# The first half of wq loaded by two DMAs, 16 partitions and then 112

## The chip, the cores and the metric

The kernel runs on one core of a Trainium2 chip. The metric is the device time of one execution in microseconds.

## The reference

One decoding step for 4 sequences: attention over a cache, and a small MLP mixer, both on the layer-normed input, summed. All data are float32.

```python
B, Sq, D = 4, 1, 512;  H, Sk, Dh = 32, 4096, 128;  F = 1792
xn = layernorm(x)
# A: attention with cached keys and values, each (4, 32, 4096, 128)
q = (xn @ wq).reshape(B, Sq, H, Dh).transpose(0, 2, 1, 3)     # wq (512, 4096)
scores = einsum("bhqd,bhkd->bhqk", q, k_cache) * Dh ** -0.5
o = einsum("bhqk,bhkd->bhqd", softmax(scores), v_cache)
A = o.transpose(0, 2, 1, 3).reshape(B, Sq, H * Dh) @ wo       # wo (4096, 512)
# B: with one token a sequence every spatial shift leaves zeros, so x1 = xn
Bm = xn + gelu(layernorm(xn) @ w3) @ w4                       # w3 (512, 1792), w4 (1792, 512)
out = x + A + Bm
```

## The kernel before

The two caches are 268 MB each and are read once. The kernel walks through them in 32 groups of 4 heads; a group's K is a tile of 128 partitions by 64 KB, and so is its V. Three buffers of that size (`slots`: S0, S1, S2) hold everything large. K of even groups goes to S1, of odd groups to S0, and V always to S2 (the last V to S1).

All large loads are issued by SP, in one order written out by hand, and so go through one DMA queue. First come the two halves of wq (line 132), 128 partitions by 32 KB each, into S2, each with a semaphore of its own (`s_wq[0]`, `s_wq[1]`); then the two halves of K(0) (line 127); then SP waits for `d_Q`, the signal that the query is ready, since K(1) goes to S0, where the work on the query lies. Then follow K(1) (L123), V(0) (L140), and V and K in turn, each as soon as its buffer is free: V(g) after `v_free`, which PE gives when it is done with the V before, and K(g+2) after `k_free`, which DVE gives when it is done with K(g). At the end come w3, w4 and wo, the last in six pieces (L152). The input x (4 rows of 2 KB, needed at four places) comes through ACT's queue (L226).

The query is made in the first 35 us. DVE norms x (L290 to L308), transposes it (L310), and PE multiplies it with wq. PE goes through wq in four chunks c, and waits for `s_wq[0]` ahead of chunk 0 and for `s_wq[1]` ahead of chunk 2. ACT scales the product (L232), DVE transposes it and copies it to `Q` (L318, L319), which sets `d_Q`.

In each group, DVE multiplies K with the query in two halves (L332, L334) and sums over the head dimension (L337), then takes the maximum (L339 to L342). ACT makes the exponentials (L242), and PE contracts them with V (`contract`) and sums the four quarters (`outputs`). After the last group, PE multiplies the result with wo as its pieces arrive, and DVE copies the sum out (L387).

The layout of a wq half is this: partition p holds rows 4p to 4p+3 of wq, and a half is two of these rows, 32 KB that lie together both in HBM and in the buffer.

Of the kernel before, what the change touches and what calls it, by code (L numbers as in the profile page):

```python
# [13 lines left out]
P = 128  # L14
# [6 lines left out]
def decode_block(ctx: ExitStack, tc: tile.TileContext, x, k, v, wq, wo, w3, w4, out):  # L21
# [4 lines left out]
    NC = D // P  # L26
# [39 lines left out]
    def sem(name):  # L66
        return tc.alloc_semaphore(name)

    def take(e, s, n=1):
        e.wait_ge(s, n).then_inc(s, -n)  # L70
# [4 lines left out]
    s_wq = [sem(f"swq{n}") for n in range(2)]  # L75
# [16 lines left out]
    def group(flat, g):  # L92
        n = HG * S * DH
        return flat[g * n:(g + 1) * n].rearrange("(p r) -> p r", p=P)
# [8 lines left out]
    wq_sb = S2[:, :].rearrange("p (c n) -> p c n", c=NC)  # L103
# [11 lines left out]
    def mm(e, o, l, r, start, stop):  # L115
        return e.matmul(o, l, r, start=start, stop=stop)  # L116

    with tc.tile_critical(no_gpsimd_drain=True), nc.Block(no_gpsimd_drain=True) as block:

        @block.sync  # L120
        def _(e):
            def load_k(g):
                e.dma_start(KS[g % 2][:, :], group(kf, g)).then_inc(s_k[g % 2], 16)  # L123

            def load_k_half(g, n, s):
                r = slice(n * ROW // 2, (n + 1) * ROW // 2)
                e.dma_start(KS[g % 2][:, r], group(kf, g)[:, r]).then_inc(s, 16)

            wq_r = wq.rearrange("(p c) n -> p c n", p=P)
            for n in range(2):  # L130
                c = slice(n * NC // 2, (n + 1) * NC // 2)
                e.dma_start(wq_sb[:, c, :], wq_r[:, c, :]).then_inc(s_wq[n], 16)
            load_k_half(0, 0, s_k[0])
            load_k_half(0, 1, s_kh)
            e.wait_ge(d_Q, 1)
            load_k(1)
            for g in range(NG - 1):
                if g > 0:
                    take(e, v_free)
                e.dma_start(S2[:, :], group(vf, g)).then_inc(s_v, 16)  # L140
                if g + 2 < NG:
                    take(e, k_free[g % 2])
                    load_k(g + 2)
            take(e, k_free[0])
            e.dma_start(S1[:, :], group(vf, NG - 1)).then_inc(s_vl, 16)
            take(e, v_free)
            e.dma_start(w3_sb, w3.rearrange("(p c) f -> p c f", p=P)).then_inc(s_w3, 16)
            e.dma_start(w4_sb, w4.rearrange("(p m) n -> p m n", p=P)).then_inc(s_w4, 16)
            take(e, k_free[1])
            wo_r = wo.rearrange("(p c) n -> p c n", p=P)  # L150
            for n, (c0, c1) in enumerate(PIECES):
                e.dma_start(wo_sb[:, c0:c1, :], wo_r[:, c0:c1, :]).then_inc(s_wo[n], 16)  # L152
# [12 lines left out]
        @block.tensor  # L165
        def _(e):
            e.wait_ge(d_xT, 1)
            for c in range(NC):
                if c % (NC // 2) == 0:
                    e.wait_ge(s_wq[c // (NC // 2)], 16)  # L170
                w = wq_sb[:, c, :].rearrange("p (n j h d) -> p n h j d", n=2, j=JB // 2, h=HG)
                for n in range(2):
                    for h in range(HG):
                        i = mm(e, (pa, pb)[n][32 * h:32 * h + 32, :], xnT[:, c, :], w[:, n, h], c == 0, c == NC - 1)
                    if c == NC - 1:
                        i.then_inc(p_q, 1)

            def contract(V):
                for g in range(G4):
                    t = g % 4  # L180
                    i = mm(e, pv[32 * t:32 * t + 32, :], pw[:, g, :], V[:, 4 * g:4 * g + 4, :], g < 4, g >= G4 - 4)
                return i

            def outputs(done):
                i = mm(e, oz[:, HG:2 * HG], ones[:, :], rs[:, :], True, True)
                if done is not None:
                    i.then_inc(done, 1)
                take(e, a_os)
                for m in range(4):
                    i = mm(e, oz[:, 0:HG], os[:, m, :], sel[:, HG * m:HG * m + HG], m == 0, m == 3)  # L190
                i.then_inc(p_oz, 1)

            def spread(b):
                take(e, d_lt)
                mm(e, pa[:, 32 * b:32 * b + 32], lt[:, :, :], sel[:, :], True, True).then_inc(p_x, 1)

            with nc.Fori(0, NG - 1, 1, engines=[ET.PE]):
                take(e, s_v, 16)
                take(e, a_w)
                contract(V3).then_inc(p_pv, 1)  # L200
                outputs(v_free)
            for b in range(B - 1):
                spread(b)
            take(e, a_w)
            e.wait_ge(s_vl, 16)
            contract(VL).then_inc(p_pv, 1)
            e.wait_ge(s_w3, 16)
            for c in range(NC):
                for t in range(4):
                    i = mm(e, pb[32 * t:32 * t + 32, :FT], x1T[:, c, :], w3_sb[:, c, t * FT:(t + 1) * FT],  # L210
                           c == 0, c == NC - 1)
            i.then_inc(p_up, 1)
            outputs(None)
            spread(B - 1)
            mm(e, total[:, 0:P], ident[:, :], base[:, :], True, False)
            e.wait_ge(s_w4, 16)
            e.wait_ge(d_g, 1)
            for m in range(NF):
                t = m % 4
                mm(e, y[32 * t:32 * t + 32, :], gT[:, 32 * m:32 * m + 32], w4_sb[:, m, :], m < 4, False)  # L220
# [145 lines left out]
    with tc.tile_critical(no_gpsimd_drain=True):  # L366
        e = nc.tensor
# [53 lines left out]
```

## Time and profile before

| | |
|---|---|
| time, median of 3 runs | 1305.53 us (1305.29 to 1305.79) |
| the profiled execution | 1305.59 us |
| its span | 1303.7 us |
| DVE busy | 1168.0 us, 90% |
| PE busy | 363.5 us, 28% |
| ACT busy | 98.6 us, 8% |
| SP's DMA queue | 561.00 MB, 99.5% of 16 engines' span |
| mean DMA rate | 430 GB/s |

The span is the time between the first and the last recorded instruction; the execution's time also has what lies around it. A busy time counts an engine's own instructions, not its waits. The share of the DMA queue is the time that its packets took, over the span of 16 DMA engines. "Landing" is the time from the issue of a transfer to the arrival of its last part, so it includes the time that the transfer stood in the queue behind others.

### The profile page before, as it was taken

How to read it: one execution, taken by the hardware profiler on the slowest of the kernel's cores; microseconds unless marked ns; L12 is line 12 of the kernel's file. 1: busy time of each engine (PE TensorE's matmuls, PEld its weight loads, DVE VectorE, ACT ScalarE, POOL GpSimd, SP SyncE). 2: the span in 40 equal slices, each digit the busy share in tenths (PEclk: the TensorE clock that was granted, in tenths of full speed). 3: DMA queues.
4: the chain of work that ended last, by engine and by line, in shares of the span. 5: the costliest groups of instructions: out<-in, count | busy, mean ns of one | idle time of the engine just before them, and what ended most of it. 6: DMA issues, size and time to landing. Idle time of an engine off the chain costs nothing. (4 is left out here: it accounts for less than half of the span.)

```text
span 1303.7 us, 7006 instructions
## 1 busy us (share of the span) xinstructions
PE 363.5 (28%) x2622; PEld 130.8 (10%) x2622; DVE 1168.0 (90%) x340; ACT 98.6 (8%) x334; POOL 2.1 (0%) x9
## 2 busy tenths in 40 slices
PE   3032123333113333213333212333311333321246
PEld 0010001111001111001111000111100111100112
DVE  3999999999999999999999999999999999999971
ACT  0000000000000000000000000000000000000010
POOL 0000000000000000000000000000000000000000
PEclk9565566666566666556666556666556666655669
DMA  9999999999999999999999999999999999999998
GB/s 403 435 445 424 444 422 442 426 440 426 436 432 432 436 430 438 424 444 422 446 422 446 423 440 426 438 430 438 428 438 430 430 438 428 440 424 444 422 431 342
DMA packets 10870, 561.11 MB, mean 430 GB/s; under 512 B 1232, under 2 KB 1248, under 8 KB 1520
## 3 DMA queue, kind: packets, MB, share of 16 engines
q1 hardware_dynamic: 10816, 561.00, 99.5%
q8 instruction: 3, 0.05, 0.0%
q10 hardware_dynamic: 48, 0.04, 0.0%
q14 instruction: 3, 0.02, 0.0%
HBM read 561.02 MB, written 0.01 MB: 430 GB/s over the span
## 5 line engine op out<-in xcount | busy, mean ns | idle before, releaser
L337 DVE TENSOR_REDUCE sc<-slot 128x128 f32<-128x16384 f32 x32 | 551.0, 17220 | 8.2 <-DVEq L70 8.2
L116 PE MATMUL ps<-slot,pw 128*32 128x512 f32 x2048 | 292.6, 736 | 878.7 <-PEq L70 878.7
L332 DVE TENSOR_TENSOR slot<-slot,qb 128x8192 f32<-128x8192 f32 x32 | 278.2, 8692 | 40.5 <-DVEq L70 40.5
L334 DVE TENSOR_TENSOR slot<-slot,qb 128x8192 f32<-128x8192 f32 x32 | 277.9, 8685 | 0.0
L116 PEld LDWEIGHTS ps<-slot,pw 128*32 128x32 f32 x2048 | 81.0, 132 | 1064.9 <-issue 1064.8
L242 ACT ACTIVATE pw<-sc,st 32x128 f32<-32x128 f32 x128 | 67.3, 526 | 247.8 <-ACTq L70 246.3
L248 ACT COPY os<-ps 128x512 f32<-128x512 f32 x31 | 18.1, 585 | 846.9 <-ACTq L70 846.9
L116 PE MATMUL ps<-sel,os 128*128 128x4 f32 x256 | 32.8, 252 | 17.5 <-PEq L70 17.5
L116 PEld LDWEIGHTS ps<-sel,os 128*128 128x128 f32 x256 | 31.0, 191 | 19.3 <-issue 19.3
L242 ACT ACTIVATION_READ_ACCUMULATOR pw<-sc,st 32x1 f32 x128 | 26.1, 204 | 0.0
L116 PE MATMUL ps<-slot 128*32 128x512 f32 x92 | 14.9, 792 | 23.7 <-DVE slot L310 22.5
L329 DVE STREAM_TRANSPOSE qb<-qx 128x128 f32<-128x128 f32 x32 | 10.0, 311 | 4.7
L387 DVE COPY res<-ps 128x128 f32<-128x128 f32 x1 | 0.3, 292 | 15.5 <-PE ps L116 15.5
L339 DVE TENSOR_REDUCE st<-sc 128x1 f32<-128x128 f32 x32 | 9.2, 286 | 4.7
L116 PE MATMUL ps<-rs,ones 128*128 128x4 f32 x64 | 12.3, 263 | 0.0
L116 PEld LDWEIGHTS ps<-rs,ones 128*128 128x128 f32 x64 | 9.5, 188 | 26.7 <-issue 26.7
L357 DVE TENSOR_TENSOR slot<-slot 128x448 f32<-128x448 f32 x1 | 0.6, 626 | 12.9 <-ACT slot L267 12.9
L326 DVE COPY qx<-Q 128x128 f32 x32 | 7.3, 227 | 4.8 <-issue 4.6
L290 DVE TENSOR_REDUCE st<-slot 128x1 f32<-128x512 f32 x2 | 1.4, 686 | 11.4 <-DMA slot<-in_A_x_dram 11.4
L341 DVE STREAM_TRANSPOSE mt<-mx 128x32 f32<-128x32 f32 x32 | 6.8, 211 | 4.7
L342 DVE TENSOR_REDUCE st<-mt 128x1 f32<-128x32 f32 x32 | 6.0, 186 | 4.8 <-DVEq L70 1.7
L340 DVE COPY mx<-st 128x32 f32<-128x32 f32 x32 | 5.8, 182 | 4.7
(56 smaller groups left out, 56.4 us busy)
## 6 DMA issues: line engine op xcount, KB each, us to landing
slot<-in_A_wq_dram SPq DMA_DIRECT2D x2, 4096.0 KB, 17.2
slot<-in_A_k_cache_dram SPq DMA_DIRECT2D x2, 4096.0 KB, 35.7
slot<-in_B_w_dram SPq DMA_DIRECT2D x2, 3584.0 KB, 22.8
slot<-in_A_wo_dram SPq DMA_DIRECT2D x3, 2048.0 KB, 30.1
slot<-in_A_wo_dram SPq DMA_DIRECT2D x1, 1024.0 KB, 36.5
slot<-in_A_wo_dram SPq DMA_DIRECT2D x1, 768.0 KB, 37.9
slot<-in_A_v_cache_dram SPq DMA_DIRECT2D x32, 28.9
slot<-in_A_k_cache_dram SPq DMA_DIRECT2D x31, 42.3
```

The costliest lines, as they stand in the source:

```text
L116: return e.matmul(o, l, r, start=start, stop=stop)
L242: i = e.activation(o, sc[r, :].rearrange("p (g w) -> p g w", w=4), AF.Exp, bias=st[r, 1:2], scale=1.0, accum_out=rs[r, h:h + 1])
L248: e.copy(os[:, :, :], pv[:, :].rearrange("p (m d) -> p m d", m=4)).then_inc(a_os, 1)
L326: own(e.tensor_copy(qx[:, :].rearrange("p (h r) -> p h r", h=4), Q[:, bass.ds(g + n, 1), :].rearrange("p o h -> p (o h)").unsqueeze(2) .to ...
L329: own(e.transpose(qb[:, :], qx[:, :]))
L332: e.tensor_tensor(out=K[:, :C // 2, :], in0=K[:, :C // 2, :], in1=qw, op=ALU.mult).then_inc(d_self, 1)
L334: e.tensor_tensor(out=K[:, C // 2:, :], in0=K[:, C // 2:, :], in1=qw, op=ALU.mult).then_inc(d_self, 1)
L337: e.reduce_sum(sc[:, :], K, axis=AX.X).then_inc(d_self, 1)
L339: own(e.reduce_max(st[:, 0:1], sc[:, :], axis=AX.X), 2)
L340: own(e.tensor_copy(mx[:, :], st[:, 0:1].to_broadcast([P, 32])))
L341: own(e.transpose(mt[:, :], mx[:, :]))
L342: e.tensor_reduce(st[:, 1:2], mt[:, :], axis=AX.X, op=ALU.max, negate=True).then_inc(d_m, 1)
```

## The change

The first half of wq is loaded by two DMAs instead of one: partitions 0 to 15 first, then partitions 16 to 127. Both add 16 to the same semaphore, and PE waits for 32 instead of 16 ahead of its first chunk. The second half is loaded as before. SP thus issues three loads for wq instead of two; nothing else is changed, and the instructions of the other engines and their order stay as they are.

```diff
             for n in range(2):
                 c = slice(n * NC // 2, (n + 1) * NC // 2)
-                e.dma_start(wq_sb[:, c, :], wq_r[:, c, :]).then_inc(s_wq[n], 16)
+                for r in ((slice(0, 16), slice(16, P)), (slice(0, P),))[n]:
+                    e.dma_start(wq_sb[r, c, :], wq_r[r, c, :]).then_inc(s_wq[n], 16)
             load_k_half(0, 0, s_k[0])
...
                 if c % (NC // 2) == 0:
-                    e.wait_ge(s_wq[c // (NC // 2)], 16)
+                    e.wait_ge(s_wq[c // (NC // 2)], 16 if c else 32)
```

## The prediction

> **What bounds the kernel now.** I read the page of the profile first: the span, the busy times, the DMA slices and the queues.
>
> ```profile
> span 1303.7 us, 7006 instructions
> ...
> PE 363.5 (28%) x2622; PEld 130.8 (10%) x2622; DVE 1168.0 (90%) x340; ACT 98.6 (8%) x334; POOL 2.1 (0%) x9
> ...
> DMA  9999999999999999999999999999999999999998
> GB/s 403 435 445 424 444 422 442 426 440 426 436 432 432 436 430 438 424 444 422 446 422 446 423 440 426 438 430 438 428 438 430 430 438 428 440 424 444 422 431 342
> ...
> q1 hardware_dynamic: 10816, 561.00, 99.5%
> ...
> slot<-in_A_wq_dram SPq DMA_DIRECT2D x2, 4096.0 KB, 17.2
> slot<-in_A_k_cache_dram SPq DMA_DIRECT2D x2, 4096.0 KB, 35.7
> ```
>
> SP's queue q1 moves 561.00 MB and occupies the 16 DMA engines for 99.5% of the span; the busiest compute engine, DVE, has 90%. To see whether the transfer rate is the limit or only follows what is asked for, I cut the span into stretches (the view of windows).
>
> ```profile
> core 0: us, PE busy (x) PEld busy (x) DVE busy (x) ACT busy (x) POOL busy (x), PEclk, DMA share, GB/s
> 0.00:10.00 10.00, 0.00 (x0) 0.00 (x0) 0.74 (x4) 0.00 (x0) 2.09 (x9) 1.00 0.84 333
> 10.00:20.00 10.00, 0.00 (x0) 0.00 (x0) 2.75 (x6) 1.58 (x2) 0.00 (x0) 1.00 1.02 441
> ...
> 60.00:300.00 240.00, 63.85 (x444) 23.04 (x444) 230.48 (x62) 19.33 (x68) 0.00 (x0) 0.61 1.00 433
> 300.00:600.00 300.00, 84.57 (x592) 30.56 (x592) 281.63 (x66) 20.76 (x72) 0.00 (x0) 0.62 1.00 433
> 600.00:900.00 300.00, 78.08 (x550) 28.04 (x554) 277.52 (x73) 22.11 (x78) 0.00 (x0) 0.61 1.00 434
> 900.00:1200.00 300.00, 78.90 (x568) 28.99 (x560) 277.77 (x72) 22.86 (x80) 0.00 (x0) 0.62 1.00 434
> ```
>
> From 60 to 1200 us the share is 1.00 and the rate 433 to 434 GB/s in every stretch. So the queue runs without a gap at a fixed rate, about 433/16 = 27.1 GB/s for each engine. The chain that ended last says the same of the end:
>
> ```profile
> 1260.99 37.90 DMA slot<-in_A_wo_dram
> 1298.89 0.04 issue
> 1298.93 1.10 PE ps L116 x32
> ...
> 1300.06 0.29 DVE res L387
> ```
>
> The last byte of wo lands at 1298.89 and what follows is a fixed tail. The program's time is therefore: start of the queue, plus bytes per engine over its rate, plus the tail. **Time that an engine loses while the queue is full is not won back; time lost anywhere else is free until it empties the queue.** The change touches the first 4 MB of that queue. The profiled execution took 1305.59 us, 1.9 over its span, and the median of the runs is 1305.53, so I work on 1305.6.
>
> **The change part by part.** Where the touched transfers lie, from the answers on the lines L132 and L127 and from the timeline:
>
> ```profile
> L132 SPq DMA_DIRECT2D slot<-in_A_wq_dram x2: 402/412/421, 1.0 to 1.4; - x2
> ...
> DMA to landing us min/median/max: 12.6/17.2/21.8
> ```
>
> ```profile
> L127 SPq DMA_DIRECT2D slot<-in_A_k_cache_dram x2: 425/490/554, 1.9 to 2.4; - x2
> ...
> DMA to landing us min/median/max: 31.0/35.7/40.3
> ```
>
> ```profile
> 1.50 1.75 ACTq L226 DMA_DIRECT2D slot<-in_A_x_dram  x4
> ...
> 14.82 0.69 DVE L290 TENSOR_REDUCE st<-slot 128x1 f32<-128x512 f32 x1 [11.37 <-DMA slot<-in_A_x_dram]
> ...
> 22.54 9.80 PE L116 MATMUL ps<-slot 128*32 128x512 f32 x64 [22.54 <-DVE slot L310]
> ...
> 34.74 0.33 SPq L123 DMA_DIRECT2D slot<-in_A_k_cache_dram  x1
> ...
> 35.11 0.43 SPq L140 DMA_DIRECT2D slot<-in_A_v_cache_dram  x1
> ...
> 35.91 8.69 DVE L332 TENSOR_TENSOR slot<-slot,qb 128x8192 f32<-128x8192 f32 x1 [0.26 <-DVEq L70]
> 44.52 8.68 DVE L334 TENSOR_TENSOR slot<-slot,qb 128x8192 f32<-128x8192 f32 x1
> ...
> 73.04 8.69 DVE L332 TENSOR_TENSOR slot<-slot,qb 128x8192 f32<-128x8192 f32 x1 [0.26 <-DVEq L70]
> ```
>
> *One more issue on SP.* A wq issue takes 0.41 us, so the second half of wq and K's two halves are issued some 0.4 us later. At 1.4 us the engines have just begun on 4 MB, which landed at 1.0 + 12.6 = 13.6; the small first block keeps them busy for 1.2 us at least, and the next issue follows in 0.4. Cost 0; without that cover, 0.4 us. ACT's x issues are on another queue.
>
> *The wait for 32.* It stands in place of the wait for 16, ahead of PE's first matmul, which today starts at 22.54, held by DVE's transpose at L310 and not by wq, landed 9 us earlier. Behind it on PE stand the query's matmuls, and for those wait ACT, DVE's copy of Q and, through d_Q, SP's loads of K(1) and V(0). Were the first half to land 9 us late, that wait would just begin to count, and the later one for the second half (landed at 1.4 + 21.8 = 23.2) would push K(1)'s issue from 34.74 to about 39 with 8.5 us on it: 23.2 + 8.5, half of PE's 9.80, and the 2.4 from PE's end at 32.3 to that issue. The two halves of K(0) are in the queue until 2.4 + 40.3 = 42.7, and would be late by the same amount; so the queue does not run dry. Cost 0; its cover is the 42.7 − 34.7 = 8 us.
>
> *The rows themselves: the term that decides.* A half of wq is 4096 KB, 32 KB in each of 128 rows. At 433 GB/s it takes 9.7 us; the landings agree (13.6, 23.2, then 32.9 and 42.7 for K's halves). Of 128 rows, each of 16 engines takes 8, so one row is 1.21 us. After the change each engine can take one row of the 16 and seven of the 112: the same 8 row times in all, if a row costs the same wherever it lies. But all long transfers of this trace are of full height, where 16 engines write to rows spread over the whole SBUF; none shows how fast 16 neighbouring rows take data. If each engine's full-height share of 8 rows stands for one path into SBUF, neighbouring rows can share a path. Bounds for the 16 rows: 1 row time (16 paths) to 8 (two paths of 8 rows). Bounds for the 112, in which engines no longer hold their accustomed rows and can meet on a path, two engines then going at half speed: 7 row times to 14. A saving below 1 + 7 is excluded as long as the engine's rate of 27.1 GB/s holds, which it does in every stretch above. No row is nearer to one end, so I take the middles, 4.5 and 10.5: 15 row times in place of 8, and 7 × 1.21 = +8.5 us on the slowest engine.
>
> [...]
>
> *Where the loss goes.* It is at the head of a queue that stays full to the end. DVE first: with K(0) 8.5 us late (first half at 41.4, second at 51.2), its first product starts 5.5 us later and the second waits some 1.2 us more, 6.7 in all. Does DVE then become the bound? Its waits at L332, in the stretch 34 to 300 us and in 600 to 1200:
>
> ```profile
> DVE slot L332 <- DVEq L70: 2.1, 8, 0.3
> ```
>
> ```profile
> DVE slot L332 <- DVEq L70: 26.7, 16, 1.8
> ```
>
> Early on DVE waits for nothing (0.26 us each); later it waits 26.7/16 = 1.7 us a group for K. It is the faster one and catches up with the queue, so its delay is swallowed and the queue's is not. Next, whether the queue still gets its orders in time:
>
> ```profile
> slot<-in_A_k_cache_dram SPq DMA_DIRECT2D x31, 42.3
> ```
>
> ```profile
> 562.53 0.33 SPq L123 DMA_DIRECT2D slot<-in_A_k_cache_dram  x1
> ...
> 595.99 0.33 SPq L140 DMA_DIRECT2D slot<-in_A_v_cache_dram  x1
> ```
>
> K ordered at 562.53 lands about 42.3 later, at 604.8; the V behind it is ordered at 595.99. The queue has 8.8 us in hand, the slowest engine most of all. An engine that is ahead by less than that never idles, and one that idles is not the slowest. So the whole loss reaches the end: 1305.6 + 8.5 = 1314.1, and I predict 1314.
>
> **The rivals.** A difference under 0.2%, 2.6 us, can't be told from none here.
>
> *First block only.* The 16 rows collide (4 row times, an estimate between the bounds 1 and 8), the 112 rows spread well and take 7: +3 × 1.21 = 3.6 us, 1309.2. For it: 112 rows reach nearly all of SBUF. Against it: the engines leave the first block at different times and with other rows than usual. Chance 0.18.
>
> *No change.* The place of a row doesn't matter, or each row still goes by the engine that has it in a full-height transfer (the split then does not spread the 16 rows over 16 engines, but 16 + 112 rows add up to the old 8 for each). The queue stays full: 1305.6, up to 0.4 more. For it: same bytes, and 99.5% of the queue untouched. [...] Chance 0.17.
>
> *One engine's queue, or one narrow path all through.* The 16 rows go at a single engine's 27.1 GB/s: 16 × 1.21 = 19.4 us instead of 1.2, +18; were the 112 rows dealt out in turn so that neighbours always meet on a quarter of the paths, 7 × 4 + 4 = 32 row times, +29. 1324 to 1335. Against it: a 4 MB transfer today shows no such lane. Chance 0.07.
>
> *Faster.* The split sets the engines out of step, and out of step they meet less in HBM, so that the queue moves at 434 GB/s where it now has 433. That is 561/0.433 − 561/0.434 = 3.0 us, 1302.6; it decides from a mean of 433.9 on. Against it: 433 to 434 stands in every stretch, whatever K and V do, like a ceiling. An earlier start can't do it: the first 10 us move 333 instead of 433 GB/s, 2.3 us of transfer in all, less than 2.6. Chance 0.03.
>
> **How the numbers follow.** The forecast (both blocks collide) keeps 0.55. Its own range is 1309.2 (the 112 at 7.0, the 16 at 4) to 1318 (4.5 + 14 row times, +12.7). The first two rivals pull the lower end to 1305.2; left out are the narrow path and the faster case, 0.10, and what the forecast has above its middle bounds. Slower: 0.55 + 0.18 + 0.07 = 0.80; same 0.17; faster 0.03.
>
> **What would show it.** In the changed profile: the first 20 us move fewer GB/s (333 and 441 now), by 8.5 × 433 = 3.7 MB in all over the first 30 us; both wq landings and K's halves are 8 or 9 us late; the second DVE product waits; x lands later than 14.8, since its small packets take turns with slower big ones; the stretches from 60 to 1200 stay at 433 to 434 and the last byte lands at about 1307.4. Wrong would be: landings of K's halves unchanged (no change), a loss that shows only in the first 10 us and is 3 to 4 us (first block only), a loss that DVE or the queue's reserve swallows by 300 us, or a steady rate above 434.

## The result, and the profile after

The changed kernel takes 1314.92 us (median; 1314.56 to 1314.98 over 6 runs), the kernel before 1305.43 us in the same comparison: **9.5 us slower, ratio 1.0072, interval 1.0062 to 1.0082.** Line numbers in the changed kernel are one higher from L133 on.

The page of the changed kernel, the lines that answer to those shown of before:

```profile
span 1313.1 us, 7007 instructions
...
PE 370.0 (28%) x2622; PEld 132.1 (10%) x2622; DVE 1167.9 (89%) x340; ACT 98.6 (8%) x334; POOL 2.1 (0%) x9
...
q1 hardware_dynamic: 10832, 561.00, 99.5%
...
slot<-in_A_k_cache_dram SPq DMA_DIRECT2D x2, 4096.0 KB, 44.5
...
slot<-in_A_wq_dram SPq DMA_DIRECT2D x1, 4096.0 KB, 30.7
slot<-in_A_wq_dram SPq DMA_DIRECT2D x1, 3584.0 KB, 21.4
...
slot<-in_A_wq_dram SPq DMA_DIRECT2D x1, 512.0 KB, 7.1
```

The span has grown by 9.4 us and the queue moves the same 561.00 MB. It still occupies the engines for 99.5% of the span: the share counts the time that packets take, whether they go fast or slowly, so the share alone would not show the loss. The packets went up by 16 (10816 to 10832), with the one DMA more. The windows show the rate itself (columns as in the prediction, DMA share and GB/s last). After, the first four stretches and two later ones:

```profile
0.00:10.00 10.00, 0.00 (x0) 0.00 (x0) 0.74 (x4) 0.00 (x0) 2.09 (x9) 1.00 0.88 158
10.00:20.00 10.00, 0.00 (x0) 0.00 (x0) 0.00 (x0) 0.00 (x0) 0.00 (x0) 1.00 1.01 264
20.00:30.00 10.00, 0.00 (x0) 0.00 (x0) 4.57 (x11) 1.58 (x2) 0.00 (x0) 1.00 0.92 368
30.00:40.00 10.00, 9.55 (x64) 2.25 (x64) 5.94 (x16) 0.89 (x2) 0.00 (x0) 1.00 1.06 455
...
60.00:300.00 240.00, 65.01 (x444) 23.16 (x444) 231.22 (x56) 17.20 (x60) 0.00 (x0) 0.60 1.00 435
300.00:600.00 300.00, 79.88 (x550) 28.43 (x554) 278.84 (x73) 22.11 (x78) 0.00 (x0) 0.59 1.00 434
```

Before, the stretch missing in the prediction's table is this:

```profile
20.00:30.00 10.00, 7.46 (x44) 1.86 (x48) 7.78 (x22) 0.29 (x1) 0.00 (x0) 1.00 1.00 433
```

In the first 30 us the queue moved 10 × (333 + 441 + 433) = 12.07 MB before and 10 × (158 + 264 + 368) = 7.90 MB after. The missing 4.17 MB are 9.6 us at 433 GB/s, the whole difference. From 60 us on the rate is as before. The end of the chain in the changed kernel:

```profile
1270.33 37.93 DMA slot<-in_A_wo_dram
1308.26 0.04 issue
1308.30 1.10 PE ps L116 x32
...
1309.42 0.29 DVE res L388
```

The last byte lands at 1308.26 instead of 1298.89, 9.4 us later, and the tail behind it is unchanged.

### The profile page after: what moved, and what is told of

It is laid out like the page before. It is cut to its first block, busy times and chain, and to the rows that moved or that the text cites. A ratio compares the mean times of both kernels' runs of the same rounds, so it can differ in the third digit from the quotient of the medians.

```text
span 1313.1 us, 7007 instructions
## 1 busy us (share of the span) xinstructions
PE 370.0 (28%) x2622; PEld 132.1 (10%) x2622; DVE 1167.9 (89%) x340; ACT 98.6 (8%) x334; POOL 2.1 (0%) x9
## 3 DMA queue, kind: packets, MB, share of 16 engines
q1 hardware_dynamic: 10832, 561.00, 99.5%
## 5 line engine op out<-in xcount | busy, mean ns | idle before, releaser
L116 PE MATMUL ps<-slot,pw 128*32 128x512 f32 x2048 | 298.8, 749 | 875.6 <-PEq L70 875.6
L333 DVE TENSOR_TENSOR slot<-slot,qb 128x8192 f32<-128x8192 f32 x32 | 278.2, 8692 | 42.3 <-DVEq L70 42.3
L249 ACT COPY os<-ps 128x512 f32<-128x512 f32 x31 | 18.1, 585 | 865.9 <-ACTq L70 865.9
L116 PE MATMUL ps<-sel,os 128*128 128x4 f32 x256 | 32.8, 252 | 17.5 <-PEq L70 17.5
L388 DVE COPY res<-ps 128x128 f32<-128x128 f32 x1 | 0.3, 290 | 14.8 <-PE ps L116 14.8
L358 DVE TENSOR_TENSOR slot<-slot 128x448 f32<-128x448 f32 x1 | 0.6, 624 | 13.6 <-ACT slot L268 13.6
L116 PEld LDWEIGHTS ps<-rs,ones 128*128 128x128 f32 x64 | 9.5, 188 | 26.7 <-issue 26.7
## 6 DMA issues: line engine op xcount, KB each, us to landing
slot<-in_A_wq_dram SPq DMA_DIRECT2D x1, 3584.0 KB, 21.4
```

The source lines that it names most:

```text
L249: e.copy(os[:, :, :], pv[:, :].rearrange("p (m d) -> p m d", m=4)).then_inc(a_os, 1)
L333: e.tensor_tensor(out=K[:, :C // 2, :], in0=K[:, :C // 2, :], in1=qw, op=ALU.mult).then_inc(d_self, 1)
```

## Experiments

Each kernel differs from the kernel before by the edit shown; the semaphore's wait ahead of PE's first use is raised to match, 16 for each DMA. Times are medians; the kernel before stood at 1305.38 to 1305.47 us beside them.

**Two DMAs of full height.**

```diff
-                e.dma_start(wq_sb[:, c, :], wq_r[:, c, :]).then_inc(s_wq[n], 16)
+                for m in (range(2), (c,))[n]:
+                    m = slice(m, m + 1) if n == 0 else m
+                    e.dma_start(wq_sb[:, m, :], wq_r[:, m, :]).then_inc(s_wq[n], 16)
```

> The first half of wq in two full-height DMAs, one row of wq (16 KB a partition) each; PE waits for 32. Theory P (paths into SBUF): what costs is that the rows of one DMA share paths; full height keeps each engine on its own path, so no cost: 0 to +0.5 us against before, 1305.4 to 1306. Theory N (each more DMA ahead of the queue costs by itself): +9 as with the split by partitions, 1314.5. Theory M (where rows that one DMA reads lie in HBM sets the cost): full height reads rows from all over wq, so 0.

Measured: 1305.52 us, ratio 1.0001 (0.9991 to 1.001). A second DMA costs nothing by itself; theory N is out.

**Two halves of 64 partitions.**

```diff
+                for d, r in ([(slice(b, b + 64),) * 2 for b in (0, 64)], ((slice(0, P), slice(0, P)),))[n]:
+                    e.dma_start(wq_sb[d, c, :], wq_r[r, c, :]).then_inc(s_wq[n], 16)
```

> The first half of wq in two DMAs of 64 partitions, 0 to 63 and 64 to 127; PE waits for 32. [...] Theory N: +9 too. Theory U (only uneven splits hurt, since 7 rows an engine set the engines out of step with their paths): 0, 1305.4.

Measured: 1316.35 us, +11.0. An even split costs more than the uneven one (9.5); theory U is out.

**Eight blocks of 16 neighbours, and eight combs of every eighth partition.** The list of rows above becomes

```diff
+                for d, r in ([(slice(b, b + 16),) * 2 for b in range(0, P, 16)], ...)[n]:   # blocks
+                for d, r in ([(slice(b, P, 8),) * 2 for b in range(8)], ...)[n]:            # combs
```

> The first half of wq in eight DMAs of 16 neighbouring partitions; PE waits for 128. Theory P with four paths for 16 neighbours: each block takes 4 row times instead of 1, 32 in place of 8, so +29 us, 1334. If a block costs what the first block of the changed kernel seems to have cost (3 us over its even share), +24, 1329. Theory N: eight DMAs, 7 more, +63, 1368. Theory U: 0.

> The first half of wq in eight DMAs of 16 partitions each, every eighth one (b, b+8, ... b+120); PE waits for 128. [...] If 16 rows a DMA are slow wherever they lie: the same as eight blocks, +24 to +29. Theory M: rows read from all over wq, 0. Theory N: +63.

Measured: blocks 1332.61 us, +27.2; combs 1316.34, +11.0. Both have eight DMAs of 16 rows and the same bytes; only which partitions stand together differs. The windows show the rates while these transfers run. Blocks, then combs, both from 10 to 20 us:

```profile
10.00:20.00 10.00, 0.00 (x0) 0.00 (x0) 0.00 (x0) 0.00 (x0) 0.00 (x0) 1.00 1.05 120
```

```profile
10.00:20.00 10.00, 0.00 (x0) 0.00 (x0) 4.58 (x11) 1.58 (x2) 0.00 (x0) 1.00 0.99 207
```

A quarter of 433 is 108 and a half is 217. 16 neighbours go at little over a quarter of the rate (120, and 135 in the next 10 us), the combs and (205 GB/s in the same stretch) the halves of 64 at nearly half of it. That fits theory P if 16 neighbours have about a quarter of the paths that full height has, and the combs and the halves about half; these two shares are my estimate from the rates. The four paths in the expectation of the blocks stood on no run when it was written, and no view shows a path. With exactly a quarter and a half, 8 row times become 32 and 16, and 1.21 us for each one added makes 29 us for the blocks and 9.7 for the combs and the halves; 27.2 and 11.0 were measured. Why the sizes miss these sums stays open. The row of the halves:

```profile
10.00:20.00 10.00, 0.00 (x0) 0.00 (x0) 0.00 (x0) 0.00 (x0) 0.00 (x0) 1.00 0.99 205
```

One more reading has to be put aside: few rows could simply occupy few engines. The share speaks against it. It is 1.05 in the blocks and 0.99 in the combs and the halves, as at the full rate; if a quarter of the engines worked at their usual pace, it would be about a quarter. From share and rate, one row of 32 KB takes an engine 16 × 32.8 KB × 1.02 / 441 GB/s = 1.2 us before, and by the same sum 4.6 us in the blocks and 2.5 us in the combs and the halves: by this the engines are all occupied, and each row takes longer.

**Reads or writes?** In the two kernels above the rows read and the rows written go together. Two more take them apart: neighbours written and spread rows read, then the mirror. Both leave out that each row of wq must stand on its own partition, so their query is another one; the transfers are as many and as large.

```diff
+                for d, r in ([(slice(16 * b, 16 * b + 16), slice(b, P, 8)) for b in range(8)], ...)[n]:
+                for d, r in ([(slice(b, P, 8), slice(16 * b, 16 * b + 16)) for b in range(8)], ...)[n]:
```

> Eight DMAs again, each writes a block of 16 neighbouring partitions (16b to 16b+15) but reads 16 rows spread over all of wq (b, b+8, ...); so the rows of wq stand on other partitions and the query is another one, with amount and instructions unchanged. Theory P (the written partitions set the cost): as the eight blocks, +27 us, 1332.6. Theory M (the place of the rows read in HBM sets it): as the eight combs, +11, 1316.3.

> The mirror of it: each of eight DMAs reads 16 neighbouring rows of wq and writes every eighth partition; the rows of wq stand on other partitions again. Theory P: as the eight combs, +11 us, 1316.3. Theory M: as the eight blocks, +27, 1332.6. If both sides count, something between or above.

Measured: 1332.42 us (+27.0) with spread reads, 1316.41 (+11.0) with spread writes. The time follows the partitions written and not the rows read, and the stretch from 10 to 20 us says the same, first spread reads, then spread writes:

```profile
10.00:20.00 10.00, 0.00 (x0) 0.00 (x0) 0.00 (x0) 0.00 (x0) 0.00 (x0) 1.00 1.13 130
```

```profile
10.00:20.00 10.00, 0.00 (x0) 0.00 (x0) 4.57 (x11) 1.58 (x2) 0.00 (x0) 1.00 1.01 214
```

Theory M is out: the limit is on the side of the SBUF.

**The 112 rows first.** Only the order of the two DMAs is turned.

> The 112 rows (partitions 16 to 127) first, the 16 rows after them. Theory P: the same rows share the same paths in another order, about the same loss, +8 to +10.5 us, 1313.4 to 1316. If the loss of the 112 comes only from engines that leave the 16 out of step: the 112 at 7 row times, the 16 at 4, +3.6, 1309.

Measured: 1314.68 us, +9.3. The 112 rows are slow without the 16 ahead of them too. They land 18.1 us after their issue, at 19.1:

```profile
slot<-in_A_wq_dram SPq DMA_DIRECT2D x1, 3584.0 KB, 18.1
```

Seven even rows would have landed at about 13.6 − 1.2 = 12.4, so the 112 lose 6.7 us with no block ahead of them. Nor does the loss need the 16 rows behind them. In the first 10 us the kernel before moves 3.33 MB, less than the 3.67 MB of the 112 rows, so the 16 rows can hardly have begun by then. Yet the rate is already 224 GB/s instead of 333, at the same share of 0.84:

```profile
0.00:10.00 10.00, 0.00 (x0) 0.00 (x0) 0.74 (x4) 0.00 (x0) 2.09 (x9) 1.00 0.84 224
```

**Elsewhere in the queue.** The same split on w3, near the end, and then on the second half of wq, once as 16 + 112 and once as eight blocks:

```diff
-            e.dma_start(w3_sb, w3.rearrange("(p c) f -> p c f", p=P)).then_inc(s_w3, 16)
+            for r in (slice(0, 16), slice(16, P)):
+                e.dma_start(w3_sb[r], w3.rearrange("(p c) f -> p c f", p=P)[r]).then_inc(s_w3, 16)
```

> wq is loaded as before; instead w3, near the end of the queue (128 partitions by 28 KB, rows that follow one another in HBM), is loaded by a DMA of 16 partitions and one of 112; PE waits for 32. Theory P, with the loss in a full queue never won back: 28/32 of the changed kernel's +9.5, +8.3 us, 1313.7. If the loss belongs to the start of the queue, where nothing is in flight yet: 0. If the 64 KB pitch of wq's rows in HBM has a part in it: less than +8.3.

Measured: 1315.89 us, +10.5. The loss is not one of the queue's start: 1250 us later, with rows that follow one another in HBM, it is as large, and none of it is won back. It looks larger than the 8.3 us of the bytes, though the interval of these two runs (ratio 1.005 to 1.0109) holds both. So a test of why:

```diff
+                for r in ((slice(0, P),), (slice(0, 16), slice(16, P)))[n]:
+                    e.dma_start(wq_sb[r, c, :], wq_r[r, c, :]).then_inc(s_wq[n], 16)
```

> The second half of wq is split 16 + 112 instead of the first, so the same rows of 32 KB meet a queue that already runs. Why did the split of w3, 28/32 of the bytes, cost 10.5 us and not 8.3? Theory S: at the start of the queue some of the loss lies beside the slow first rows that the kernel before has there anyway (333 GB/s in its first 10 us, 2.3 us lost); then the split costs more here than at the start, 10.3 to 12, 1315.7 to 1317.4. Theory W (something of w3 itself, its 28 KB rows or the end of the queue, where engines are further out of step): +9.4 as in the first half, 1314.8.

> The second half of wq in eight blocks of 16 neighbouring partitions. Four paths for 16 rows make 32 row times in place of 8: +29.1 us, 1334.5, if nothing of it is hidden; in the first half it was +27.2. Theory S: +29 or more. Theory W: +27.2, 1332.6.

Measured: the split 1316.11 us, +10.6 (ratio 1.0081, 1.0064 to 1.0098), in the range of theory S; the eight blocks 1333.11, +27.6, between the two expectations and too coarse to tell them apart (1.0191 to 1.0232). The split in the second half costs 1.1 us more than in the first; the intervals of the two ratios overlap, but none of its four runs (1315.95 to 1316.18) comes near the six of the changed kernel (1314.56 to 1314.98). The landings of the split second half show something that neither theory had:

```profile
slot<-in_A_wq_dram SPq DMA_DIRECT2D x1, 4096.0 KB, 15.5
slot<-in_A_wq_dram SPq DMA_DIRECT2D x1, 3584.0 KB, 31.9
slot<-in_A_wq_dram SPq DMA_DIRECT2D x1, 512.0 KB, 18.6
```

The first half, of full height and issued ahead of the split, lands 15.5 us after its issue instead of 12.6; ahead of the eight blocks it takes 15.0. With w3 split, the last two V land 37.4 us after their issue in the median instead of 35.7; if the earlier of them takes its 29.0 us as before, the last V, which is just ahead of w3 in the queue, takes an estimated 45.8 instead of 42.4. That fits engines that finish the transfer ahead early, go on to the 16 rows and take paths that late engines still need; no view shows the engines one by one, so this is argued and not shown. At the start of the queue there is no transfer ahead. How the 1.1 us between the two places divide between this and the slow start of theory S is open, and so is the rest of w3's excess (28/32 of 10.6 would be 9.3, and 10.5 was measured).

## Why the prediction was right, point by point

*The bound* held. The loss at the head arrived whole at the end: K's halves landed 9.3 and 9.2 us late (at 2.3 + 39.9 = 42.2 and 2.9 + 49.0 = 51.9, by the row below, against 32.9 and 42.7), the last byte 9.4 us late, the program 9.5 us later.

```profile
L127 SPq DMA_DIRECT2D slot<-in_A_k_cache_dram x2: 564/582/600, 2.3 to 2.9; - x2
...
DMA to landing us min/median/max: 39.9/44.5/49.0
```

*The issue and the wait* cost nothing, as said; but not by the rows named. In the changed kernel's timeline:

```profile
22.73 0.69 DVE L291 TENSOR_REDUCE st<-slot 128x1 f32<-128x512 f32 x1 [19.28 <-DMA slot<-in_A_x_dram]
...
30.44 9.55 PE L116 MATMUL ps<-slot 128*32 128x512 f32 x64 [30.44 <-DVE slot L311]
...
42.38 0.33 SPq L123 DMA_DIRECT2D slot<-in_A_k_cache_dram  x1
...
43.55 8.69 DVE L333 TENSOR_TENSOR slot<-slot,qb 128x8192 f32<-128x8192 f32 x1 [0.26 <-DVEq L70]
52.16 8.68 DVE L335 TENSOR_TENSOR slot<-slot,qb 128x8192 f32<-128x8192 f32 x1
```

x landed 7.9 us later (22.7 instead of 14.8), which the text named as a sign and left out of its sum for the query. So PE's first matmul was late by x and not by wq (the first half was there at 1.4 + 21.4 = 22.8), K(1) was issued at 42.38 instead of the expected 39, and DVE's first product began at 43.55, held by the query, where I had put 41.4, held by K(0). The second product, which was to wait, did not: K(0) had landed at 51.9 and it began at 52.16. None of this reached the end. K(1) was ordered 9.5 us before K(0)'s last landing, a reserve even wider than the 8 us of before, since the queue moved back by more than the query.

*DVE swallowed its delay*: its waits at L333, in the stretches 34 to 300 and 600 to 1200 us, are as before (2.1 and 26.7 us), so later on it waits for K again:

```profile
DVE slot L333 <- DVEq L70: 1.8, 7, 0.3
```

```profile
DVE slot L333 <- DVEq L70: 26.6, 16, 1.8
```

*The rows, the term that decides*: +8.5 us forecast, 9.5 measured, inside the range of 1309.2 to 1318. Where the rows are written decides, as forecast: neighbours cost 27.0 us where the same number of spread rows cost 11.0. That fits rows that share paths, though no view shows one. The size was in part luck. Eight blocks cost 27.2 us, 3.4 each, so 16 neighbours take 1 + 3.4/1.21 = 3.8 row times where I took 4.5. No run shows the 4 row times at the lower end of the range, nor the quarter of the paths in the rival of the narrow path; in their place the blocks showed 3.8 row times and 120 of 433 GB/s. If the first block of the split cost as much, 6.1 us are left for the 112, 7 + 5.0 = 12 row times where I took 10.5; with the 112 ahead, they lost 6.7. Both lie within their bounds, 1 to 8 and 7 to 14. Each middle was taken for want of a nearer row; one was 0.7 too high and the other 1.5 too low, and the two errors partly cancel.

*The spread between engines* hardly shows. The forecast put its 8.5 us on the slowest engine, which left room for others to be less late. The missing 4.17 MB are 9.6 us as a mean over all engines, and K's last landing, which waits for the slowest, is 9.2 us late: the engines came out about equally late. Which engine takes which of the 112 rows, no view shows; that their loss comes from meeting on a path is argued from the experiments with 16 and 64 rows.

*The rivals.* No change, and faster, fell with the first result; no change falls with the two halves of 64 as well, which cost 11.0 us more than one DMA of 128. First block only gave 1309.2, and the 112 cost more than the 16. The narrow path all through would have shown 108 GB/s to 30 us; the changed kernel's rates rise to 264 from 10 to 20 us.

## What to carry to other kernels

A load that names part of the partitions can be much slower than one of all 128: here 120 of 433 GB/s for 16 neighbours and 205 for 64. Naming nearly all of them is not enough: the 112 ran at 264, from 10 to 20 us in the changed kernel. To cut a large load in pieces, cut it along the free dimension at full height; that cost nothing here (1305.52 us against 1305.38). In a kernel whose queue is full from the first byte to the last, such a loss comes out at the end: 9.5, 10.6 and 10.5 us at the three places tried.

## What the runs showed that I had not expected

With a DMA that covers part of the partitions behind it, a transfer of full height lands later too: 4 MB took 15.5 us instead of 12.6. And 112 rows of 128, which reach nearly all of the SBUF, lost about 6 us where seven even row times take 8.5: an estimated 6.1 behind the block of 16, 6.7 ahead of it.
